# Fused attention and gated product on one core: a first set of plain block products, and weight work moved from GpSimd to VectorE

## The chip, the cores and the metric

The kernel runs on one core of a Trainium2 chip. The metric is the device time of one execution in microseconds (us). A core has a matrix engine (TensorE; PE in the profile, with its weight loads as PEld), three elementwise engines (VectorE or DVE, ScalarE or ACT, GpSimd or POOL) and SyncE (SP), whose queue issues most of the DMA transfers; ScalarE's queue can issue them too. Each engine takes its instructions in the order in which they were written, and they wait for each other by semaphores.

## The reference

Attention with a position bias comes first, then a gated product without a nonlinearity:

```python
def _attn_ref(q, k, v, w1, b1, w2):          # q, k, v: (8, 8, 576, 64)
    scores = scale * np.matmul(q, k.transpose(0, 1, 3, 2)) + bias(w1, b1, w2)
    attn = softmax(scores)
    return np.matmul(attn, v)
def _moe_ref(x, w1, w2, w3, w_out):          # x: (4608, 512)
    a = x @ w1                               # 512 x 1024
    b = x @ w2                               # 512 x 1024
    h = a * b @ w3                           # 1024 x 1024
    return h @ w_out                         # 1024 x 512
```

x is the attention's output, 8 x 576 tokens of 512 values. The change touches the second function alone.

## The kernel before, in words

**First half: attention** (to L592). 32 units, one for each pair of heads and batch, run one behind another in a periodic order written as tables of times. Each leaves its output in DRAM (`x_d`, L444) without the softmax's division; the reciprocals go to DRAM too (`r_d`, L357 and L358). Between the units the weights w_out and w3 are brought in. They come as 64-bit floats, and `narrow` (L144) makes 32-bit floats of them in eight steps: fetch (DMA into `wi`), size and rest (ScalarE), clamp, shift, head and power (VectorE: L172, L178, L188, L194), and total (L199 and L200, two tensor steps on GpSimd).

**The fold.** w3 and w_out are multiplied once on the core to one matrix of 1024 x 512 (`fold`, L630; 16 steps of 12 matmuls, L653). Numbers go to TensorE as a high and a low part, each in a form of reduced precision: high x high, high x low, low x high make three matmuls of one. ScalarE makes the high parts (a copy into that form), another engine the low part (the number less its high part). `evict_w` (L657) puts the results, again as high and low parts, where w3 was.

**Second half: six sets of 768 tokens** (`NPR` = 6, `TOK` = 768). A set's x (512 features x 768 tokens, `xr`) is loaded by `load_x` (L665), together with the reciprocals `rb` (L674), and scaled by `split_x` (L680): steps r0 to r3 scale, S1 to S4 are sums of quarters, h0 to h6 and l0 to l6 are seven high and low parts. Seven products take the place of eight (Winograd's form of Strassen's scheme for 2 x 2 blocks): the blocks are two halves of the tokens by two halves of the features on one side, and w1 and w2 by two halves of the features on the other. So the weights need four sums too (`sums_w`, L718, on GpSimd, 256 elements a partition each) and high and low parts of seven blocks (`split_w`, L725: high on ScalarE, low on GpSimd, L732, one step of 768 and one of 1024 elements).

A set has eight **turns**, one for each 128 of the 1024 columns (`NF` = 8), so there are 48 turns. In a turn TensorE makes the products P1, P2, P6, P5, P7, P3, P4 (`product`, L736; six matmuls of 384 columns each, L748) in two PSUM banks, and between them the six steps D0 to D5 of the turn before (`down`, L798; three matmuls of 512 columns, L805), which multiply with the folded matrix. `finish` (L757) copies and adds what stands in the banks (ScalarE L764, VectorE L767), multiplies both branches (g) and splits the result (gh on ScalarE L777, gl on VectorE). The weight sums and splits of turn n + 1 are made in turn n. Of the 16 weight pieces of w1 and w2 (`prep_w`, L611) six are made during the fold, the other ten in the first turns. At a set's first turn the set before is stored (`store`, L809): ScalarE copies a bank to one of two buffers (`wos6`, `wos7`), SyncE sends it.

**What sets the order.** Every step has a time in a plan (the constants at L26 to L57); `drive` (L205) sorts by it and writes the instructions of TensorE, ScalarE, VectorE and GpSimd in that order. On the chip only the order remains. SyncE's order is set by the scheduler, not by the plan.

Of the kernel before, what the change touches and what calls it, by code (L numbers as in the profile page):

```python
# [18 lines left out]
P = 128  # L19
# [27 lines left out]
L_X = 7 * STEP
ENDS_X = {
    "S3": L_X + 1.25, "S4": L_X + 2.90, "h2": L_X + 4.62, "l2": L_X + 5.60, "h3": L_X + 6.30, "l3": L_X + 7.40, "h4": L_X + 7.20,
    "l4": L_X + 9.65, "h5": L_X + 8.10, "l5": L_X + 11.50, "h6": L_X + 11.45, "l6": L_X + 12.70,  # L50
}
BEGIN_X = {"r0": 2.90, "r1": 4.70, "r2": 2.90, "r3": 4.70, "S1": 2.90, "S2": 4.70, "h0": 4.62, "h1": 6.30, "l0": 2.90, "l1": 4.70}
NEXT_X = (
    dict(ENDS_X, **{n: d + STEP * (3 + k // 2) for k, (n, d) in enumerate((n, BEGIN_X[n]) for n in ("r0", "r1", "r2", "r3", "S1", "S2", "l0", "l1"))},
         h0=5 * STEP + 6.3, h1=5 * STEP + 7.2),
    dict(ENDS_X, **dict(zip(("r0", "r1", "r2", "r3", "S1", "S2", "l0", "l1"), (5 * STEP + d for d in FREE_D))), h0=5 * STEP + 6.3, h1=5 * STEP + 7.2),
)  # L57
# [36 lines left out]
def relpos_attention_moe(  # L94
# [49 lines left out]
    def narrow(pool, src, n, x, queue, pieces=1, low=nc.scalar, both=True):  # L144
# [53 lines left out]
        def total():  # L198
            nc.gpsimd.tensor_tensor(x, x, f(d["power"]), op=ALU.mult)  # L199
            nc.gpsimd.tensor_tensor(x, d["mag"], x, op=ALU.add)  # L200
# [410 lines left out]
    def prep_w(pool, t, m):  # L611
# [18 lines left out]
    def fold(t, hf):  # L630
# [15 lines left out]
        (nc.gpsimd if hf and t % 2 else nc.vector).tensor_tensor(w3l, w3s[t][hf], f(w3h), op=ALU.subtract)  # L646
# [18 lines left out]
    def load_x(c, queue):  # L665

        X = sets[c]["X"] = xs.tile([P, NC, TOK], F32, name="xr", bufs=1)
        sets[c]["rb"] = []
        for cc in range(NC):
            queue.dma_start(X[:, cc, :], x_d[cc][:, c * TOK:(c + 1) * TOK])  # L670
# [301 lines left out]
```

## Time and profile before

| | |
|---|---|
| median of 3 runs | 1169.37 us (1169.08 to 1169.75) |
| profiled execution | 1172.74 us |
| its span, first to last instruction | 1171.0 us |
| mean granted clock of TensorE | 0.973 |
| busy: PE, DVE, ACT, POOL | 1089.6, 859.6, 697.6, 746.9 us |
| DMA over the span | 123.22 MB, mean 105 GB/s |

The page of the profile gives busy time by engine, a picture of the span in slices, the chain of work that ended last, and groups of instructions. A group's row names the source line, engine, operation, tiles (out<-in) and shapes, the count, the busy time, the mean duration in ns, and the idle time of the engine just before them with what ended it. A timeline's row gives the start and the duration in us; a bracket is idle time before it and what ended that. The table of windows gives busy time and count by engine in a stretch, then the granted clock, the share of DMA time and GB/s. A busy TensorE is not one at its peak, since pipelined matmuls overlap.

### The profile page before, as it was taken

What the parts mean: (1) busy time and instruction counts of PE and PEld (TensorE: products, weight loads), DVE (VectorE), ACT (ScalarE), POOL (GpSimd) and SP (SyncE); (2) the same over time, 40 slices, a digit from 0 to 9 for tenths busy, and PEclk for the clock granted to TensorE, in tenths of its full rate; (3) what the DMA queues carried; (4) which work ended last, traced back from release to release, by engine and by line L of the source; (5) the groups of instructions that cost most, each with busy time, mean ns of one, the idle gap of its engine ahead of it and who ended that gap; (6) DMA issues with size and microseconds to landing.
All of it is one profiled execution on the core that took longest, in us unless ns stands there. A gap on an engine that the chain in (4) does not pass through costs nothing.

```text
span 1171.0 us, 23840 instructions
## 1 busy us (share of the span) xinstructions
PE 1089.6 (93%) x9380; PEld 907.0 (77%) x9380; DVE 859.6 (73%) x1459; ACT 697.6 (60%) x1337; POOL 746.9 (64%) x542
## 2 busy tenths in 40 slices
PE   7769999999999999967788899999999999999997
PEld 3247778777777777645577789998998998999996
DVE  8948987997899799649699665784882784587333
ACT  6769988998998899633443263444354344335342
POOL 0337765775777576435789767785875776586750
PEclk9989999999999999988889899999999999999999
DMA  6954573556457354152221130121103103001001
GB/s 204 310 168 146 165 246 119 180 172 226 140 172 245 115 161 137 58 163 90 90 71 38 54 108 18 38 70 39 54 2 108 55 1 108 28 1 55 1 1 54
DMA packets 58159, 123.22 MB, mean 105 GB/s; under 512 B 9152, under 2 KB 19264, under 8 KB 58048
## 3 DMA queue, kind: packets, MB, share of 16 engines
q1 hardware_dynamic: 55568, 117.59, 31.8%
q10 hardware_dynamic: 2480, 4.11, 1.3%
q8 instruction: 74, 1.21, 0.4%
q14 instruction: 37, 0.30, 0.1%
HBM read 91.76 MB, written 29.92 MB: 104 GB/s over the span
## 4 chain that ended last, share of the span: by engine, by line
PE 74%; DMA 6%; POOL 4%; ACT 3%; DVE 3%; issue 2%; SPq 0%; ACTq 0%; DVEq 0%; POOLq 0%
PE up L748 26%; PE o L805 14%; PE pst L431 14%; PE s L311 12%; PE pst L368 6%; DMA out_dram<-wos 3%; DMA wi<-in_moe_w_dram 2%; POOL wt L723 2%; POOL wu L199 1%; POOL url L732 1%; DVE xr L693 1%; DMA x_d<-x 1%; DMA rb<-r_d 1%; PE wacc L653 1%; ACT pt L393 1%
## 5 line engine op out<-in xcount | busy, mean ns | idle before, releaser
L748 PE MATMUL up<-xch,urh 128*128 128x384 f32 x672 | 233.1, 347 | 24.6 <-ACT wos L764 14.8
L322 DVE CUSTOM_DVE_ANT_0 ts<-s,nb 128x576 f32<-128x576 f32 x288 | 210.7, 754 | 48.2 <-PE s L311 21.5
L748 PE MATMUL up<-xcl,urh 128*128 128x384 f32 x672 | 229.8, 342 | 0.0
L748 PE MATMUL up<-xch,url 128*128 128x384 f32 x672 | 229.5, 341 | 0.0
L347 ACT ACTIVATE pp<-ts,mx 128x576 f32<-128x576 f32 x256 | 195.8, 770 | 20.5 <-DVE mx L322 18.8
L767 DVE TENSOR_TENSOR wos<-up,wos 128x384 f32<-128x384 f32 x144 | 78.2, 551 | 171.3 <-PE up L748 160.6
L732 POOL TENSOR_TENSOR url<-wu,urh 128x768 fp32r<-128x768 f32 x48 | 90.5, 1886 | 151.7 <-ACT urh L734 151.7
L805 PE MATMUL o<-w3s,gh 128*128 128x512 f32 x576 | 183.5, 400 | 0.0
L431 PE MATMUL pst<-pt,rv 128*64 128x256 f32 (+1 forms) x1280 | 167.5, 407 | 1.6 <-DVE rt L391 1.4
L748 PEld LDWEIGHTS up<-xch,urh 128*128 128x128 f32 x672 | 128.7, 192 | 44.0 <-ACT wos L764 18.9
L777 ACT ACTIVATE gh<-g 128x384 fp32r<-128x384 f32 x96 | 50.5, 526 | 161.2 <-DVE g L767 159.8
L764 ACT COPY wos<-up 128x384 f32<-128x384 f32 x144 | 68.1, 477 | 118.9 <-PE up L748 118.9
L393 ACT ACTIVATE pt<-pst 128x1024 f32<-128x1024 f32 x128 | 124.0, 1018 | 21.6 <-PE pst L368 21.6
L748 PEld LDWEIGHTS up<-xch,url 128*128 128x128 f32 x672 | 128.6, 191 | 10.4
L431 PEld LDWEIGHTS pst<-pt,rv 128*64 128x64 f32 x1280 | 87.6, 136 | 63.2 <-issue 9.0
L732 POOL TENSOR_TENSOR url<-wt,urh 128x1024 fp32r<-128x1024 f32 x48 | 132.6, 2763 | 0.0
L311 PE MATMUL s<-kh,qh 64*128 64x288 f32 x640 | 118.5, 366 | 11.6 <-DVE mx L322 11.4
L748 PEld LDWEIGHTS up<-xcl,urh 128*128 128x128 f32 x672 | 128.2, 191 | 0.0
L805 PE MATMUL o<-w3s,gl 128*128 128x512 f32 x288 | 115.5, 401 | 0.4 <-DVE gl L767 0.4
L805 PEld LDWEIGHTS o<-w3s,gh 128*128 128x128 f32 x576 | 106.9, 191 | 4.9
L368 PE MATMUL pst<-ident,pp 64*128 64x64 f32 x2304 | 102.1, 223 | 0.8 <-ACT pt L393 0.8
L368 PEld LDWEIGHTS pst<-ident,pp 64*128 64x128 f32 x2304 | 97.0, 139 | 6.5 <-ACT pt L393 5.7
(105 smaller groups left out, 2261.8 us busy)
## 6 DMA issues: line engine op xcount, KB each, us to landing
rq<-in_q_dram SPq DMA_DIRECT2D x31, 640.0 KB
wi<-in_moe_w_dram SPq DMA_DIRECT2D x32, 512.0 KB
nb_d<-bev SPq DMA_DIRECT2D x36, 295.5 KB
rv<-in_v_dram SPq DMA_DIRECT2D x32, 320.0 KB
x_d<-x SPq DMA_DIRECT2D x32, 288.0 KB
rk<-in_k_dram SPq DMA_DIRECT2D x31, 288.0 KB
rb<-r_d SPq DMA_DIRECT2D x44, 192.0 KB
xr<-x_d SPq DMA_DIRECT2D x20, 384.0 KB
```

Of the source, the lines that this page charges most:

```text
L311: nc.tensor.matmul(s[:, hf, :HS], Q[x][rows, q0:q0 + P], K[y][rows, h * HS:(h + 1) * HS], start=(m == 0), stop=(m == len(ops) - 1),)
L322: nc.vector.tensor_tensor_reduce(out=halves(ts), in0=d.pop(("s", t))[:, :, :HS], in1=halves(NB[p, t]), op0=ALU.add, op1=ALU.min, scale=-1. ...
L347: nc.scalar.activation(pp, ts, AF.Exp, bias=mx, scale=-1.0, accum_out=sums[p][:, 9 * b + col:9 * b + col + 1])
L368: nc.tensor.transpose(ps[0:n, hf, c0:c0 + 64], x[rows], ident[rows, rows])
L393: nc.scalar.activation(o, x, AF.Copy)
L431: nc.tensor.matmul(o, x[:, c0:c0 + D], m, start=(c == 0), stop=(c == 4 and n_m == len(ms) - 1),)
L732: nc.gpsimd.tensor_tensor(l[:, rows], src, f(h[:, rows]), op=ALU.subtract)
L748: nc.tensor.matmul(acc, l[:, b, ks], r[:, k], start=(m == 0 and which in ("P1", "P2", "P5")), stop=(m == 3 * KH - 1), skip_group_check=whi ...
L764: nc.scalar.copy(d[name], d[src])
L767: nc.vector.tensor_tensor(o, a, b, op=op)
L777: nc.scalar.activation(d["gh"][:, i * CH:(i + 1) * CH], d["g"][:, i], AF.Copy)
L805: nc.tensor.matmul(d["o", t], l[:, sl], folded[ft][r], start=(ft == 0 and m == 0), stop=(ft == NF - 1 and m == 2),)
```

## The change

- The first set (c = 0, turns 0 to 7) is made of eight plain block products: `plain`, named A0, A1 (w1) and B0, B1 (w2) by token half, 12 matmuls of 384 columns each. It needs four high and low parts of x in place of seven, no sums of x or of weights, and weight splits of four blocks (1024 elements) in place of seven.
- `sums_w`, the low part in `split_w`, and `total` of the w1 and w2 pieces are on VectorE. All low parts of w3 in the fold are, too; GpSimd keeps those of w_out.
- Four weight pieces are made during the fold in place of six. The other twelve follow in the first turns at 0.6 and 7.6 us of a turn.
- The first x and r are loaded from SyncE's queue (before: ScalarE's), all four r at once, two of them into tiles that the sums of x use later.
- `store` goes through five buffers (`wos3` to `wos7`) in place of two. The copies in `finish` use three (`wos0` to `wos2`) in place of two sets of three.
- The tables of times are rewritten: when x of the next set is scaled, added and split, and where the weight steps stand in a turn.

The diff, cut to its core (the tables of times are shown by two lines):

```diff
-PROD, DOWN, STEP = 1.05, 0.682, 11.44
+FULL, HALF = 12.63, 11.57
+TURN_F = (("A0", 0.00), ("D0", 2.11), ("D1", 2.81), ("B0", 3.51), ("D2", 5.62), ("A1", 6.32), ("D3", 8.43), ("B1", 9.13), ("D4", 11.24), ("D5", 11.94))
...
         def total():
-            nc.gpsimd.tensor_tensor(x, x, f(d["power"]), op=ALU.mult)
-            nc.gpsimd.tensor_tensor(x, d["mag"], x, op=ALU.add)
+            add.tensor_tensor(x, x, f(d["power"]), op=ALU.mult)
+            add.tensor_tensor(x, d["mag"], x, op=ALU.add)
...
-        return narrow(cv, src, NC * P, x, nc.sync, pieces=NC)
+        return narrow(cv, src, NC * P, x, nc.sync, pieces=NC, add=nc.vector)
...
-        (nc.gpsimd if hf and t % 2 else nc.vector).tensor_tensor(w3l, w3s[t][hf], f(w3h), op=ALU.subtract)
+        nc.vector.tensor_tensor(w3l, w3s[t][hf], f(w3h), op=ALU.subtract)
...
         for cc in range(NC):
-            queue.dma_start(X[:, cc, :], x_d[cc][:, c * TOK:(c + 1) * TOK])
-            if cc < 2:
-                load_r(c, cc, queue)
+            nc.sync.dma_start(X[:, cc, :], x_d[cc][:, c * TOK:(c + 1) * TOK])
+            if cc < 2 or c == 0:
+                load_r(c, cc)
...
+        if c == 0 and cc > 1:
+            rb = xs.tile([P, KH, CH], F32, name=f"s{cc - 1}", bufs=1).rearrange("p k n -> p (k n)")
+        else:
+            rb = xs.tile([P, TOK], F32, name="rb", bufs=2)
...
-            nc.gpsimd.tensor_tensor(o, a, b, op=ALU.subtract)
+            nc.vector.tensor_tensor(o, a, b, op=ALU.subtract)
...
-        src, rows = ((B[:, 1:4], slice(0, 3)), (d["T"], slice(3, 7)))[part]
+        if n < NF:
+            src, rows = B, slice(0, 4)
+        else:
+            src, rows = (d["T"], slice(3, 7)) if part else (B[:, 1:4], slice(0, 3))
         if low:
-            nc.gpsimd.tensor_tensor(l[:, rows], src, f(h[:, rows]), op=ALU.subtract)
+            nc.vector.tensor_tensor(l[:, rows], src, f(h[:, rows]), op=ALU.subtract)
...
+    def plain(n, which):
+        d, x = turns[n], sets[0]["x"]
+        m, t = "AB".index(which[0]), int(which[1])
+        acc = d[which] = ps_up.tile([P, 512], F32, name=f"up{m}")[:, 0:CH]
+        wh, wl = d["w"]
+        for k in range(KH):
+            for j in range(KH):
+                b, js = 2 - 2 * m + k, slice(j * P, (j + 1) * P)
+                xh, xl = x[2 * t + k]
+                for i, (l, r) in enumerate(((wh, xh), (wl, xh), (wh, xl))):
+                    nc.tensor.matmul(
+                        acc, l[:, b, js], r[:, j], start=(k == j == i == 0), stop=(k == j == KH - 1 and i == 2),
+                    )
...
-        o = held.tile([P, DO], F32, name=f"wos{6 + t % 2}")
+        o = held.tile([P, DO], F32, name=f"wos{3 + (c * NT + t) % 5}")
...
-    add(later, end + 0.05, lambda: load_x(0, nc.scalar))
+    add(later, end + 0.05, lambda: load_x(0))
...
+    begin = [t_f + min(n, NF) * FULL + max(n - NF, 0) * HALF for n in range(NSTEP + 1)]
+    for i in range(len(EARLY_W), 2 * NF):
+        n, k = divmod(i - len(EARLY_W) + 1, len(FREE_W))
+        put_w(plan, wpool, i, begin[n] + FREE_W[k] - 6.0, begin[n] + FREE_W[k])
```

How instructions stand now, at three places. ScalarE around the load of the first x, before (`x` is the last attention output's copy, `xr` and `rb` the loads, `wmag` a weight piece, `w3h` the fold's high parts, `w3s<-wacc` the first folded results):

```order
L393 ACTIVATE x<-pst 128x320
L644 ACTIVATE w3h<-w3s_87 128x512
L670 DMA xr<-x_d_98 128x768
L678 DMA rb<-r_d_102 64x768 x2
L670 DMA xr<-x_d_99 128x768
L678 DMA rb<-r_d_103 64x768 x2
L670 DMA xr<-x_d_100 128x768
L670 DMA xr<-x_d_101 128x768
L162 ACTIVATE wmag<-wi 128x512
L166 ACTIVATE wu_9068<-wi 128x512
L644 ACTIVATE w3h<-w3s_74 128x512
```

The same place after the change:

```order
L397 ACTIVATE x<-pst 128x320
L648 ACTIVATE w3h<-w3s_87 128x512
L166 ACTIVATE wmag<-wi 128x512
L648 ACTIVATE w3h<-w3s_74 128x512
L664 ACTIVATE w3s_9438<-wacc_9108 128x512
```

The loads have left ScalarE's queue, and one weight step with them. On VectorE, a turn of the first set before (`wos<-up,wos` are the additions, `g` the products, `gl` the low parts, `wmag` and `wi` a weight piece):

```order
L767 TENSOR_TENSOR wos_9822<-up_9815,wos_9822 128x384
L188 SCALAR_TENSOR_TENSOR wmag<-wi,wmag 128x512
L194 TENSOR_SCALAR wi<-wmag 128x512
L172 TENSOR_SCALAR wmag<-wmag 128x512
L178 TENSOR_SCALAR wmag<-wmag 128x512
L767 TENSOR_TENSOR wos_9873<-up_9802,wos_9873 128x384
L188 SCALAR_TENSOR_TENSOR wmag<-wi,wmag 128x512
L767 TENSOR_TENSOR wos_9850<-up_9852,wos_9850 128x384
L767 TENSOR_TENSOR g<-wos_9822,wos_9850 128x384
L194 TENSOR_SCALAR wi<-wmag 128x512
```

And after (`wu` is the piece's total, `url` the low part of the next turn's weights):

```order
L790 TENSOR_TENSOR g<-up_9772,wos_9763 128x384
L790 TENSOR_TENSOR gl<-g,gh 128x384
L176 TENSOR_SCALAR wmag<-wmag 128x512
L182 TENSOR_SCALAR wmag<-wmag 128x512
L192 SCALAR_TENSOR_TENSOR wmag<-wi,wmag 128x512
L198 TENSOR_SCALAR wi<-wmag 128x512
L203 TENSOR_TENSOR wu_9634<-wu_9634,wi 128x512
L204 TENSOR_TENSOR wu_9634<-wmag,wu_9634 128x512
L790 TENSOR_TENSOR g<-up_9824,wos_9821 128x384
L790 TENSOR_TENSOR gl<-g,gh 128x384
```

A piece's four VectorE steps stand together now, with the two of its total behind them, and the three additions are gone. On VectorE, a turn of the other sets in which x of the next set is scaled, before:

```order
L767 TENSOR_TENSOR wos_10906<-up_10899,wos_10906 128x384
L693 TENSOR_TENSOR xr<-xr,rb 128x768 x2
L767 TENSOR_TENSOR wos_10951<-up_10887,wos_10951 128x384
L767 TENSOR_TENSOR wos_10931<-up_10933,wos_10931 128x384
L767 TENSOR_TENSOR g<-wos_10906,wos_10931 128x384
L767 TENSOR_TENSOR g<-up_10887,wos_10951 128x384
L767 TENSOR_TENSOR gl<-g,gh 128x384 x2
```

And after (`wt` are the weight sums):

```order
L790 TENSOR_TENSOR wos_10945<-up_10938,wos_10945 128x384
L730 TENSOR_TENSOR wt<-wu_9636 128x256 x2
L730 TENSOR_TENSOR wt<-wu_9636,wt 128x256 x2
L742 TENSOR_TENSOR url<-wu_9636,urh 128x768
L700 TENSOR_TENSOR xr<-xr,rb 128x768
L790 TENSOR_TENSOR wos_10986<-up_10930,wos_10986 128x384
L742 TENSOR_TENSOR url<-wt,urh 128x1024
L790 TENSOR_TENSOR wos_10968<-up_10972,wos_10968 128x384
L790 TENSOR_TENSOR g<-wos_10945,wos_10968 128x384
L790 TENSOR_TENSOR g<-up_10930,wos_10986 128x384
L790 TENSOR_TENSOR gl<-g,gh 128x384
```

The four sums and two low parts stand between the additions, and the scaling of x is spread, one step between two additions.

More of the change, by code (lines that the diff above doesn't have):

```diff
@@ L47 @@
[L47 to L50, printed above, removed]
-}
[L52 to L57, printed above, removed]
+AT_E = dict(a0=2.25, g0=5.80, h0=6.40, l0=7.00, a1=8.60, g1=11.40, h1=12.00, l1=12.65)
@@ L142, in relpos_attention_moe, with narrow @@
     MOST = struct.unpack("<f", struct.pack("<I", 0x47EFFFFF))[0]
-    def narrow(pool, src, n, x, queue, pieces=1, low=nc.scalar, both=True):
+    def narrow(pool, src, n, x, queue, pieces=1, low=nc.scalar, both=True, add=nc.gpsimd):
         d = {}
@@ L752, in product, with spare @@
                 m += 1
[L754 to L755 removed]
+    def spare(i):
+        return held.tile([P, DO], F32, name=f"wos{i}")[:, 0:CH]
     def finish(n):
         d = turns[n]
[L760 removed]
         def copy(name, i, src):
[L763 removed]
+            d[name] = spare(i)
             nc.scalar.copy(d[name], d[src])
@@ L831, in relpos_attention_moe @@
                 put(later, evict_w(hf * NF // 2 + n), at + PACE_F + 0.6 * n, at + PACE_F + 0.6 * n + 0.6)
-    for n in range(EARLY):
-        put_w(later, w01, n // 2, n % 2, t_s + AT_W1 + PACE_W * n)
+    for i, (fetch, at) in enumerate(zip(EARLY_F, EARLY_W)):
+        put_w(later, w01, i, t_s + fetch, t_s + at)
     drive([e for e in later if e[0] <= end])
@@ L839, in relpos_attention_moe @@
     psw.append(fo.enter_context(tc.tile_pool(name="psw1", bufs=1, space=PSUM)))
-    assert t_s + AT_F + NF * PACE_F > end
-    plan, t_f = [], t_s + AT_F + 2 * NF * PACE_F
+    assert t_s + AT_FO + NF * PACE_F > end
+    plan, t_f = [], t_s + AT_FO + 2 * NF * PACE_F
     def add(plan, at, step):
         plan.append((at, len(plan), step))
-    add(later, end + 0.05, lambda: load_x(0, nc.scalar))
-    at = max(t_s + AT_X, end + 0.1)
     def late(at, step):
         add(later if at < t_f - 0.5 else plan, at, step)
+    add(later, end + 0.05, lambda: load_x(0))
     for n, step in split_x(0).items():
-        late(max(t_s + AT_X, end + 0.1) + FIRST_X[n], step)
-    late(t_f - 9.0, lambda: sums_w(0))
-    for p in range(2):
-        late(t_f - 9.0 + AT_WH[p], lambda p=p: split_w(0, p, False))
-        late(t_f - 9.0 + AT_WL[p], lambda p=p: split_w(0, p, True))
+        if n in FIRST_X:
+            late(t_s + AT_X0 + FIRST_X[n], step)
+    for k in range(2):
+        late(t_f - AT_W0[1] + (0.0, 1.1)[k], lambda k=k: split_w(0, 0, k == 1))
     drive(later)
@@ L892, in relpos_attention_moe @@
         if ft == 0 and c + 1 < NPR:
-            add(plan, T + 10.0, lambda c=c: load_x(c + 1, nc.sync))
+            add(plan, T + 10.0, lambda c=c: load_x(c + 1))
+            table = NEXT_X if c else LAST_X
             for name, step in split_x(c + 1).items():
-                add(plan, T + NEXT_X[c == 0][name], step)
-    T = t_f + NSTEP * STEP
+                add(plan, begin[n + table[name][0]] + table[name][1], step)
+    T = begin[NSTEP]
     for t in range(NT):
```

126 lines of the change are left out of this document (61 added, 65 removed), and 6 rows, old and new, of tables (LAST_X, NEXT_X).

## The prediction

> **What bounds the kernel now.** First I cut the span into stages with the table of windows: attention's end with the first half of the weight fold, the fold's second half, the first eight turns, turns 8 to 46, the last turn and the tail.
>
> ```profile
> core 0: us, PE busy (x) PEld busy (x) DVE busy (x) ACT busy (x) POOL busy (x), PEclk, DMA share, GB/s
> 480.00:516.40 36.40, 33.94 (x198) 23.54 (x198) 20.41 (x28) 15.89 (x27) 21.17 (x16) 1.00 0.29 84
> 516.40:567.00 50.60, 30.99 (x97) 22.59 (x97) 31.51 (x36) 18.41 (x29) 24.97 (x18) 0.77 0.42 127
> 567.00:686.10 119.10, 99.88 (x464) 88.84 (x463) 102.11 (x106) 48.19 (x81) 97.02 (x68) 0.92 0.16 49
> 686.10:1148.70 462.60, 457.20 (x2341) 422.68 (x2340) 292.62 (x339) 198.55 (x333) 315.46 (x231) 0.99 0.13 43
> ```
>
> TensorE is nearly full in the first and fourth stage. In the second it works 31.0 of 50.6 us, at a granted clock of 0.77; in the third 99.9 of 119.1 us, at 0.92, while GpSimd is busy for 97.0. Those two stages and what keeps the fourth from being full are where time can go. TensorE's timeline has the edges (start, duration):
>
> ```profile
> 480.62 0.49 PE L653 MATMUL wacc<-woh,w3l 128*128 128x512 f32 x1
> ...
> 525.30 0.80 PE L653 MATMUL wacc<-woh,w3h 128*128 128x512 f32 x1 [8.72 <-ACT w3h L644]
> ...
> 538.04 0.80 PE L653 MATMUL wacc<-woh,w3l 128*128 128x512 f32 x1 [4.09 <-DVE w3l L646]
> ...
> 567.03 0.52 PE L748 MATMUL up<-xch,urh 128*128 128x384 f32 x1
> ...
> 686.08 0.33 PE L748 MATMUL up<-xch,urh 128*128 128x384 f32 x1
> ...
> 1148.74 0.33 PE L748 MATMUL up<-xch,urh 128*128 128x384 f32 x1
> ```
>
> Turn 0 starts at 567.03, turn 8 at 686.08, turn 47 at 1148.74. Idle time in brackets shows the fold waiting 8.72 us for ScalarE. Why ScalarE was late is in its own timeline:
>
> ```profile
> 480.00 0.68 ACT L162 ACTIVATE wmag<-wi 128x512 f32<-128x512 f32 x1 [0.80 <-DMA wi<-in_moe_w_dram]
> ...
> 522.41 0.99 ACTq L670 DMA_DIRECT2D xr<-x_d  x2
> 523.50 0.66 ACT L162 ACTIVATE wmag<-wi 128x512 f32<-128x512 f32 x1 [11.73 <-DMA x_d<-x]
> ```
>
> ScalarE's own queue held the loads of X, and those stood until the store of the last attention output had landed; 11.73 us of ScalarE went there. The chain of waits (start, length) gives the store, a pair of products, one fold step, an r load:
>
> ```profile
> 488.48 2.98 PE wacc L653 x12
> ...
> 514.18 8.88 DMA x_d<-x
> ...
> 531.63 4.33 DMA rb<-r_d
> ...
> 598.29 2.76 POOL wt L723 x3
> ...
> 714.96 2.11 PE up L748 x12
> ...
> 772.89 2.11 PE up L748 x12
> ```
>
> Five turns lie between the last two rows: (772.89 - 714.96) / 5 = 11.586 us is an undisturbed turn. Eight take 92.7 us; the first eight took 119.05, with GpSimd's steps on the chain.
>
> **The durations to use.** From the groups (mean ns), then VectorE's and GpSimd's timelines:
>
> ```profile
> L732 POOL TENSOR_TENSOR url<-wu,urh 128x768 fp32r<-128x768 f32 x48 | 90.5, 1886 | 151.7 <-ACT urh L734 151.7
> L732 POOL TENSOR_TENSOR url<-wt,urh 128x1024 fp32r<-128x1024 f32 x48 | 132.6, 2763 | 0.0
> L723 POOL TENSOR_TENSOR wt<-wu 128x256 f32<-128x256 f32 x96 | 90.6, 963 | 3.2
> L723 POOL TENSOR_TENSOR wt<-wu,wt 128x256 f32<-128x256 f32 x96 | 87.7, 913 | 3.8
> L767 DVE TENSOR_TENSOR wos<-up,wos 128x384 f32<-128x384 f32 x144 | 78.2, 551 | 171.3 <-PE up L748 160.6 <-ACT wos L764 10.6
> ```
>
> ```profile
> 530.99 2.04 DVE L693 TENSOR_TENSOR xr<-xr,rb 128x768 f32<-128x768 f32 x1
> ...
> 535.35 0.43 DVE L178 TENSOR_SCALAR wmag<-wmag 128x512 int32<-128x512 int32 x1
> ...
> 537.30 0.68 DVE L646 TENSOR_TENSOR w3l<-w3s,w3h 128x512 fp32r<-128x512 f32 x1
> 537.90 0.95 DVE L693 TENSOR_TENSOR xr<-xr,rb 128x768 f32<-128x768 f32 x1
> 538.77 0.69 DVE L188 SCALAR_TENSOR_TENSOR wmag<-wi,wmag 128x512 int32<-128x512 int32 x1
> ```
>
> ```profile
> 530.33 1.89 POOL L200 TENSOR_TENSOR wu<-wmag,wu 128x512 f32<-128x512 f32 x1
> 540.05 1.87 POOL L199 TENSOR_TENSOR wu<-wu,wi 128x512 f32<-128x512 f32 x1 [7.84 <-ACT xch L702]
> ```
>
> The same multiply of 768 elements takes VectorE 2.04 us while GpSimd works (530.33 to 532.22) and 0.95 us while GpSimd is idle (until 540.05). After the change GpSimd has nothing left once the fold's low parts of w_out are made, so I use the undisturbed values: 0.43, 0.69, 0.68 (512 elements), 0.95 (768). From 0.68 and 0.95 the slope is 0.27 per 256 elements; my estimates are 0.41 for 256 and 1.22 for 1024.
>
> The Trainium skill (SBUF — State Buffer, Who interferes with whom) says that VectorE and GpSimd share one port pair as an exclusive lock, so that the second to issue blocks. The 2.04 against 0.95 agrees; were the disturbed value to hold without GpSimd, first-set turns would be VectorE-bound at about 20 us and the time would be some 60 us above my sum.
>
> **Part 1: up to turn 0.** The second half of the fold now has X's loads on SyncE's queue, so ScalarE doesn't stop; the 8.72 us goes, the cold clock with it, and no weight sums or seven-part splits stand between fold and turn 0. What is late next is TensorE itself. It was nearly full up to 516.4. One new delay: the weight piece's first steps are now ahead of the first fold's low part on VectorE. ScalarE's 480.00 to 480.68 now comes before w3h; then 0.43 + 0.46 and a 0.36 copy (my estimate of what stands ahead), and w3l from about 482.0 to 482.7, against its matmul at 480.62 now: +2.1 us. So the first half ends at 518.5. The second half is 8 steps of 12 matmuls: at most 8 x 2.98 = 23.8, and about 0.17 less each for the pipelined last matmul, 22.5; I take 22.8. Turn 0 at 541.3: **-25.7 us**. Ends: -28 (no delay at the start) and -16 (X 10 us late, below).
>
> X itself: the last attention output is stored right behind the first X load, an estimated 2 us ahead of the present 514.18; with the 8.88 us of now it lands at 521, the last X and r loads take 4.33 more, so scaling ends near 528. VectorE's low part of fold step 5, queued behind the scaling, is wanted at 518.5 + 5 x 2.85 = 532.7. Cover 4 to 5 us; if it is gone, each further us is paid.
>
> **Part 2: first set.** Eight block products are 48 matmuls of 384 columns in place of 42. Twelve take 2.11 us at most, six 1.05; a turn is 11.586 + 1.05 = 12.64, eight 101.1 against 119.05: **-17.9 us**, if TensorE stays fed. VectorE per turn: two weight pieces of 3 x 0.43 + 0.69 + 2 x 0.68 = 3.34 each, one low part 1.22, two products and two low parts of 0.55: 6.68 + 1.22 + 2.2 = 10.1 of 12.64. In turns 4 to 7 the next set's X adds up to six steps of 0.95, where a piece or both are missing: about 12.3 in turn 6. GpSimd's load now per turn is 1.89 + 2.76 + 2 x (0.96 + 0.91) = 8.4, and each of ten late pieces adds about 3: 97 in 119 us, one step waiting for the other. The new piece steps don't feed the turn that they lie in, nor the next, so a late one costs nothing until it has used most of a turn. Ends: -17.9 and 0 (pieces pace the turns as now).
>
> **Part 3: the other 40 turns.** No matmul changes. VectorE per turn: seven steps of 0.55 (3.9), four sums (1.6), 0.95 and 1.22: 7.7 of 11.586; the 15 steps of the next X (scaling, sums, low parts) add at most three of 0.95 in one turn: 10.5, and 15 x 0.95 / 8 = 1.8 in the mean. By the turn's table P5, which needs the sum of P2 (due 2.35, 0.55 long), is due at 4.56, 1.6 us later; the next turn's P2, which needs the last product (due 10.40), has 1.6 us too. The new sums stand behind the first, and nothing longer than 1.22 stands before the second. I take 0. The ends: +2.5 us a turn if VectorE took GpSimd's times (3.9 + 8.4 + 1.8 = 14.1), and no gain.
>
> The stores do change this stage: 39 turns from 686.08 to 1148.74 take 462.66, against 451.9 undisturbed: 10.8 us too many. ScalarE's waits in this stage, and those in the tail:
>
> ```profile
> ACT wos L814 <- DMA out_dram<-wos: 22.7, 15, 4.6
> ```
>
> ```profile
> 1164.80 0.37 ACT L819 COPY wos<-o 128x256 f32<-128x256 f32 x1 [0.49 <-DMA out_dram<-wos]
> ...
> 1166.63 0.37 ACT L819 COPY wos<-o 128x256 f32<-128x256 f32 x1 [1.46 <-DMA out_dram<-wos]
> ```
>
> With two store buffers the third copy waits for the first transfer, and the copies of P1 queue behind it on ScalarE. With five, only the sixth copy reuses a buffer, 9.3 us after its first use (due 12.20 and 2.90); transfers of X that stand on SyncE's queue between the stores wait only for the last low part of the present X. I take 9.5 of the 10.8 as gone (0.25 stays at each of five set starts): **-9.5 us**, ends 0 and -10.8. In the tail 0.49 + 1.46: **-2.0 us**, ends 0 and -3.
>
> **The sum.** -25.7 - 17.9 - 9.5 - 2.0 = -55.1. The profiled execution took 1172.74 us (span 1171.0): 1117.6, span 1115.9. The median of the runs lies 3.4 lower, 1169.37: **1114.3 us**.
>
> **Rivals.**
> - X late. All X and r loads and the store go through one queue now. If that brings the last r 10 us beyond its cover, turn 0 starts at 551: 1124.3. For it: 8.88 us for one store with transfers ahead of it. Against: X of a set is 1.5 MB and the window moved 127 GB/s with room left. The Trainium skill (DMA: Bandwidth & Descriptors, Queues, rings and completion order) has descriptors of one queue consumed in ring order, which speaks against merging two queues; by that rule the wait is this rival's.
> - Pieces pace the first set. Load, ScalarE, six VectorE steps, next load into the same buffer is a loop over two buffers; if it turns in 15 us a pair as now, the 17.9 is not gained: 1132.2. Against: without GpSimd the loop has 10.1 us of VectorE in 12.64.
> - The store gaps stay, because the X loads between the stores hold SyncE: 1169.37 - 45.6 = 1123.8.
> - Slower: VectorE becomes the bound of the 40 turns. It decides above 11.586 + 55.1/40 = 13.0 us a turn; at 14.1 the time is 1114.3 + 40 x 2.5 = 1214. For it: in-order VectorE now holds everything between two products. Against: 7.7 by undisturbed rows.
> - That the work isn't moved: the order of instructions shows no GpSimd row after the fold, so no chance.
>
> **How the numbers follow.** Forecast 0.60, X late 0.14, pieces 0.13, store gaps 0.09, slower 0.03, no change 0.01. The range takes the forecast's ends on the good side (-28.2 - 17.9 - 10.8 - 3.0 = -59.9, 1109.5, less 1 for what these bounds leave out) and reaches to the pieces' rival: 1108.5 to 1133. 0.2% is 2.3 us, about what a measurement tells from no change; all cases but the last two are far faster. Faster 0.96, same 0.01, slower 0.03.
>
> **What would show it.** Right: the first product near 541, turn 8 about 101 us later at a clock of 1.00, turns of 11.59 at the set starts too, ScalarE without waits on the output's transfers, VectorE some 60 to 70% busy in the seven-product turns. Wrong: TensorE idle behind w3l (X late), VectorE's pieces waiting on loads with TensorE idle on url (pieces), or sums of P2 ending later than 1.6 us after P2 (VectorE-bound).

## The result and the profile after

| | before | after |
|---|---|---|
| median of 4 runs each, same chip | 1169.22 us (1167.12 to 1169.75) | 1115.74 us (1114.10 to 1116.05) |
| ratio, 95% interval | | 0.9543 (0.9526 to 0.9559) |
| profiled execution, its span | 1172.74, 1171.0 us | 1115.74, 1113.9 us |
| mean granted clock of TensorE | 0.973 | 0.989 |
| busy: PE, DVE, ACT, POOL | 1089.6, 859.6, 697.6, 746.9 us | 1076.3, 859.5, 688.3, 302.2 us |

The change is 4.6% faster, and the forecast of 1114.3 us is 1.4 us off. In three of the comparisons below one execution ran far longer than the rest (2605.5 and 3544.4 us, and 1473.1 us of the kernel before); the ratios leave these out, and no median moves by more than 0.7 us without them.

The table of windows of the changed kernel, cut at the same places as before (attention's end with the fold's first half, the second half, the first set, turns 8 to 46):

```profile
core 0: us, PE busy (x) PEld busy (x) DVE busy (x) ACT busy (x) POOL busy (x), PEclk, DMA share, GB/s
480.00:518.40 38.40, 35.43 (x223) 25.29 (x220) 22.63 (x36) 18.98 (x35) 11.08 (x8) 1.00 0.30 88
518.40:541.10 22.70, 21.61 (x93) 17.21 (x93) 16.43 (x24) 10.52 (x17) 0.00 (x0) 1.00 0.88 191
541.10:641.90 100.80, 98.18 (x511) 90.36 (x510) 82.48 (x134) 42.38 (x73) 0.00 (x0) 1.00 0.24 79
641.90:1093.80 451.90, 451.90 (x2342) 420.53 (x2341) 333.75 (x572) 200.75 (x332) 0.00 (x0) 1.00 0.13 44
```

GpSimd is at 0 from the fold's second half on, and the clock at 1.00 in all four rows. TensorE has no idle time left in the last row and 2.6 us in the third. VectorE does more in the first set than before (134 instructions against 106) in less busy time (82.48 us against 102.11). TensorE's timeline gives the edges and the waits that are left:

```profile
482.21 0.50 PE L657 MATMUL wacc<-woh,w3h 128*128 128x512 f32 x1 [1.16 <-ACT w3h L648]
...
483.83 0.50 PE L657 MATMUL wacc<-woh,w3l 128*128 128x512 f32 x1 [0.89 <-DVE w3l L650]
...
517.52 0.39 PE L657 MATMUL wacc<-woh,w3h 128*128 128x512 f32 x1
...
533.08 0.50 PE L657 MATMUL wacc<-woh,w3l 128*128 128x512 f32 x1 [1.09 <-DVE w3l L650]
...
541.10 0.34 PE L756 MATMUL up<-xch,urh 128*128 128x384 f32 x1
...
559.54 0.44 PE L756 MATMUL up<-xch,urh 128*128 128x384 f32 x1 [0.85 <-DVE g L790]
...
641.90 0.33 PE L772 MATMUL up<-xch,urh 128*128 128x384 f32 x1
...
1093.78 0.33 PE L772 MATMUL up<-xch,urh 128*128 128x384 f32 x1
```

The second half of the fold starts at 517.52, turn 0 at 541.10, turn 8 at 641.90, turn 47 at 1093.78. From first product to first product, turns 0 to 7 take 8.35, 13.70, 12.79, 12.79, 12.79, 13.69, 13.67 and 13.03 us; all 39 from turn 8 to 47 take 11.59. Set against the forecast's terms, in the profiled executions:

| term | forecast | measured |
|---|---|---|
| turn 0 | -25.7 | 567.03 to 541.10: -25.9 |
| first set | -17.9 | 119.05 to 100.80: -18.3 |
| turns 8 to 46 | -9.5 | 462.66 to 451.88: -10.8 |
| turn 47 and the tail | -2.0 | 22.26 to 20.12: -2.1 |
| sum | -55.1 | -57.1 |

Each term is within 1.3 us, but the first set's is right by luck, by two errors that cancel: turn 0 has no steps D0 to D5 to run and takes 8.35 us, not 12.64, and the next seven take 92.45, not 88.5. What VectorE does in a turn stands in its timeline, here one turn of the first set from low part to low part of the weights:

```profile
557.79 1.23 DVE L742 TENSOR_TENSOR url<-wu,urh 128x1024 fp32r<-128x1024 f32 x1 [1.13 <-ACT urh L744]
558.93 0.55 DVE L790 TENSOR_TENSOR g<-up,wos 128x384 f32<-128x384 f32 x1
560.07 0.56 DVE L790 TENSOR_TENSOR gl<-g,gh 128x384 fp32r<-128x384 f32 x1 [0.59 <-ACT gh L796]
...
565.29 0.56 DVE L790 TENSOR_TENSOR gl<-g,gh 128x384 fp32r<-128x384 f32 x1 [0.59 <-ACT gh L796]
...
570.58 1.23 DVE L742 TENSOR_TENSOR url<-wu,urh 128x1024 fp32r<-128x1024 f32 x1 [1.13 <-ACT urh L744]
```

570.58 - 557.79 = 12.79 us is the turn. Its work is 1.23 + 2 x (0.55 + 0.56) + 2 x 3.36 for the two pieces = 10.2, as forecast. The rest is waiting: twice 0.59, while ScalarE makes gh between VectorE's g and gl, and 1.13, while it makes urh between the total and url; that is 2.3, and 0.3 are small gaps. VectorE stands idle then, with the next piece's steps queued behind. So the reading is that VectorE's order, and not TensorE, sets these turns, by handshakes (the waits for ScalarE inside one chain) that the sum left out.

This turn and its like, turns 2 to 4, are only 0.2 us longer than the 12.61 that TensorE needs (experiment 1). Of the 4.2 us that the seven turns lose against that, 3.6 lie in the other four. Turns 5 and 6 have a scaling step of the next X on VectorE as well (0.95 us each, at 602.54 and 616.21), turn 7 more of them in place of the pieces; and behind turn 0, which TensorE is through with in 8.35 us, VectorE's list is late, and TensorE waits for g in turn 1 (0.85 us at 559.54).

### The profile page after: what moved, and what is told of

The parts are those of the page before. It is cut to its first block, busy times and chain, and to the rows that moved or that the text cites. A ratio compares the mean times of both kernels' runs of the same rounds, so it can differ in the third digit from the quotient of the medians.

```text
span 1113.9 us, 23788 instructions
## 1 busy us (share of the span) xinstructions
PE 1076.3 (97%) x9428; PEld 904.2 (81%) x9428; DVE 859.5 (77%) x1712; ACT 688.3 (62%) x1318; POOL 302.2 (27%) x218
## 4 chain that ended last, share of the span: by engine, by line
PE 80%; DVE 7%; ACT 3%; DMA 2%; issue 1%; ACTq 0%; SPq 0%; DVEq 0%
PE up L772 27%; PE o L828 15%; PE pst L435 15%; PE s L315 13%; PE pst L372 6%; PE wacc L657 2%; DVE url L742 1%; DMA s<-r_d 1%; DVE wu L203 1%; DVE wmag L192 1%; DVE g L790 1%; ACT gh L796 1%; DMA xr<-x_d 1%; ACT urh L744 1%; DVE gl L790 1%
## 5 line engine op out<-in xcount | busy, mean ns | idle before, releaser
L772 PE MATMUL up<-xch,urh 128*128 128x384 f32 x560 | 189.6, 338 | 0.0
L772 PE MATMUL up<-xcl,urh 128*128 128x384 f32 x560 | 189.2, 338 | 0.0
L772 PE MATMUL up<-xch,url 128*128 128x384 f32 x560 | 188.8, 337 | 0.0
L828 PE MATMUL o<-w3s,gh 128*128 128x512 f32 x576 | 180.6, 395 | 0.0
L790 DVE TENSOR_TENSOR wos<-up,wos 128x384 f32<-128x384 f32 x120 | 66.9, 558 | 99.2 <-PE up L772 99.2
L772 PEld LDWEIGHTS up<-xch,urh 128*128 128x128 f32 x560 | 105.2, 188 | 9.2
L772 PEld LDWEIGHTS up<-xch,url 128*128 128x128 f32 x560 | 105.1, 188 | 9.0
L772 PEld LDWEIGHTS up<-xcl,urh 128*128 128x128 f32 x560 | 105.0, 188 | 0.0
L315 PE MATMUL s<-kh,ql 64*128 64x288 f32 x640 | 96.8, 296 | 2.4 <-POOL ql L299 2.4
L315 PE MATMUL s<-kl,qh 64*128 64x288 f32 x640 | 96.1, 295 | 0.0
```

What stands on the lines that cost most here:

```text
L315: nc.tensor.matmul(s[:, hf, :HS], Q[x][rows, q0:q0 + P], K[y][rows, h * HS:(h + 1) * HS], start=(m == 0), stop=(m == len(ops) - 1),)
L772: nc.tensor.matmul(acc, l[:, b, ks], r[:, k], start=(m == 0 and which in ("P1", "P2", "P5")), stop=(m == 3 * KH - 1), skip_group_check=whi ...
L790: nc.vector.tensor_tensor(o, a, b, op=op)
L828: nc.tensor.matmul(d["o", t], l[:, sl], folded[ft][r], start=(ft == 0 and m == 0), stop=(ft == NF - 1 and m == 2),)
```

## The experiments

Theory: the time went where the forecast put it, with the first set bound by VectorE's handshakes. Rivals: that one edit alone does nearly all of it, or that the parts lean on each other. Times are medians; ratios, with 95% intervals, are to the kernel before, run on the same chip beside each.

### 1. Handshakes out of the first set

The changed kernel, with the weights' high and low part and both low parts of g later in the plan of a plain turn. On VectorE two low parts come to stand elsewhere, url behind a product and the second gl behind two steps of the next piece:

```diff
-AT_E = dict(a0=2.25, g0=5.80, h0=6.40, l0=7.00, a1=8.60, g1=11.40, h1=12.00, l1=12.65)
+AT_E = dict(a0=2.25, g0=5.80, h0=6.40, l0=7.20, a1=8.60, g1=11.40, h1=12.00, l1=13.70)
-AT_RF = dict(h=3.00, l=4.20)
+AT_RF = dict(h=4.50, l=6.50)
```

> The changed kernel with VectorE's and ScalarE's order in the first set altered: the weights' low part comes behind the product g0, and the second low part of g behind the first two steps of the next piece, so that ScalarE makes the high parts while VectorE does something else. Theory: VectorE's loop falls from 12.79 to about 10.6 us a turn, TensorE becomes the bound at 12.64, and turns 1, 5, 6 and 7 lose their excess: 4 us less, 1111.5 to 1113 us. Rival, the excess comes from elsewhere (loads, TensorE itself): no change.

1111.16 us (ratio 0.9507, 0.9484 to 0.9531). Turns 1 to 7 take 12.59 to 12.61 us each, and in the table of windows the first set has TensorE full:

```profile
540.10:636.70 96.60, 96.60 (x511) 90.94 (x510) 81.28 (x136) 43.34 (x74) 0.00 (x0) 1.00 0.26 83
```

In VectorE's timeline of this kernel, the low part of g now stands behind two steps of a piece:

```profile
573.94 0.55 DVE L790 TENSOR_TENSOR g<-up,wos 128x384 f32<-128x384 f32 x1
575.63 0.43 DVE L176 TENSOR_SCALAR wmag<-wmag 128x512 f32<-128x512 f32 x1 [1.14 <-ACT wmag L166]
576.10 0.43 DVE L182 TENSOR_SCALAR wmag<-wmag 128x512 int32<-128x512 int32 x1
576.44 0.55 DVE L790 TENSOR_TENSOR gl<-g,gh 128x384 fp32r<-128x384 f32 x1
```

gl no longer waits. Over the set VectorE's waits of gl fall from 8.9 us to 0.6 and those of url from 6.3 to 2.0. VectorE still has idle time elsewhere, but it is no longer what TensorE waits for. The set shrinks from 100.80 to 96.62 us with the same instructions in another order, and turns 1, 5, 6 and 7 lose their excess with the rest; that shows the handshakes as the cause. 12.61 is also the forecast's 12.64 for a turn in which TensorE is fed. Of the 5.2 us between the two spans, 4.2 are this; the other 1.0 is that turn 0 starts at 540.08, for which experiment 2 has the reason. This version is faster than both kernels.

### 2. The fold's first step as well

The same kernel, with the first weight piece of the fold 0.6 us later in the plan, since TensorE's first fold step had waited behind it:

```diff
-EARLY_W = 1.0, 6.0, 21.0, 44.0
+EARLY_W = 1.6, 6.0, 21.0, 44.0
```

> As the run before, and the first weight piece's steps come behind the first fold step's high and low part on ScalarE and VectorE. Theory: the first half of the fold starts 2 us earlier and TensorE carries that through: another 2 us less, 1109.5 to 1111 us. Rival, TensorE waits for something else in the fold's first half: no further change.

1111.46 us (0.9505, 0.9480 to 0.9531): no further gain. In TensorE's timeline of this kernel:

```profile
480.54 0.50 PE L657 MATMUL wacc<-woh,w3h 128*128 128x512 f32 x1 [0.29 <-ACT w3h L648]
...
487.38 2.86 PE L435 MATMUL pst<-pt,rv 128*64 128x320 f32 x20 [2.00 <-DVE rt L395]
...
516.75 0.40 PE L657 MATMUL wacc<-woh,w3h 128*128 128x512 f32 x1
...
532.09 0.50 PE L657 MATMUL wacc<-woh,w3l 128*128 128x512 f32 x1 [0.88 <-DVE w3l L650]
```

The fold starts earlier, and the attention step behind it waits 2.00 us. Its second half still starts 0.8 us earlier than in experiment 1 (517.57), and gives that back at 532.09, where the low part waits 0.88 behind the scaling of X. The changed kernel shows this wait as 1.09 at 533.08, and experiment 1, where X's last r happened to land 1.0 us earlier, not at all. So in these three runs X's arrival decides turn 0 to within a microsecond.

### 3. The moved work alone

The kernel before, with the totals, sums and all low parts on VectorE; seven products in the first set, X from ScalarE's queue, two store buffers and the tables stay:

```diff
-        return narrow(cv, src, NC * P, x, nc.sync, pieces=NC)
+        return narrow(cv, src, NC * P, x, nc.sync, pieces=NC, add=nc.vector)
...
-        (nc.gpsimd if hf and t % 2 else nc.vector).tensor_tensor(w3l, w3s[t][hf], f(w3h), op=ALU.subtract)
+        nc.vector.tensor_tensor(w3l, w3s[t][hf], f(w3h), op=ALU.subtract)
...
-            nc.gpsimd.tensor_tensor(o, a, b, op=ALU.subtract)
+            nc.vector.tensor_tensor(o, a, b, op=ALU.subtract)
...
-            nc.gpsimd.tensor_tensor(l[:, rows], src, f(h[:, rows]), op=ALU.subtract)
+            nc.vector.tensor_tensor(l[:, rows], src, f(h[:, rows]), op=ALU.subtract)
```

> The kernel before with the move alone: totals of the w1 and w2 pieces, weight sums, weights' low parts and all low parts of w3 on VectorE, everything else (seven products in the first set, tables, six early pieces, x from ScalarE's queue, two store buffers) as before. Theory: five turns of the first set hold two pieces and the seven-product work on VectorE, 6.7 + 7.7 = 14.4 us and waits for ScalarE, about 15.5 us a turn, and the stall of the fold stays: 1154 to 1164 us. Rival, the move alone brings most of the gain: 1135 us or less.

1137.35 us (0.9729, 0.9701 to 0.9757), outside both and close to the rival. The move brings 32 of the 53.5 us: turn 8 starts at 659.94 instead of 686.08, and turns 8 to 46 take 452.4 instead of 462.7 us, though two store buffers are left. One reason stands in SyncE's queue. Of the kernel before:

```profile
506.42 7.66 SPq L157 DMA_DIRECT2D wi<-in_moe_w_dram  x2
514.18 0.46 SPq L444 DMA_DIRECT2D x_d<-x  x1
```

The first row of SyncE's waits between 505 and 515 us (in total, times, longest):

```profile
SPq L157 <- POOL wu L199: 13.6, 2, 6.8
```

The copy of the last attention output was done at 511.26 (it starts at 510.82 and takes 0.44). Its store left SyncE only at 514.18, since a weight load ahead of it waited until GpSimd had made a total. With the totals on VectorE, SyncE and ScalarE read:

```profile
514.03 0.34 SPq L444 DMA_DIRECT2D x_d<-x  x1
515.89 0.37 SPq L157 DMA_DIRECT2D wi<-in_moe_w_dram  x1
```

```profile
513.57 0.44 ACT L393 ACTIVATE x<-pst 128x320 f32<-128x320 f32 x1 [7.58 <-PE pst L431]
...
519.39 0.66 ACT L162 ACTIVATE wmag<-wi 128x512 f32<-128x512 f32 x1 [4.85 <-DMA rb<-r_d]
```

The store now leaves right behind its copy, and the weight load comes behind the store in SyncE's order. It doesn't leave earlier (514.03 against 514.18), since the copy itself is 2.75 us later. But ahead of it went one load of X, where two of X, four of r and the weight load had gone before, and the chain of waits has it land after 4.20 us in place of 8.88:

```profile
514.03 4.20 DMA x_d<-x
```

ScalarE stands for 4.85 us where it had stood for 11.73; 2.8 of the difference is that it starts to wait later, 4.1 that it goes on earlier (519.39 against 523.50). On TensorE the wait at this place falls from 8.72 to 1.90 us, with X's loads in ScalarE's queue as before:

```profile
521.17 0.50 PE L653 MATMUL wacc<-woh,w3h 128*128 128x512 f32 x1 [1.90 <-ACT w3h L644]
```

The window from the first product to turn 8 says what bounds the rest:

```profile
550.57:659.90 109.33, 99.91 (x486) 87.39 (x487) 101.77 (x186) 52.51 (x89) 0.00 (x0) 0.98 0.21 68
```

VectorE is busy for 101.77 of 109.33 us. This window is not the first set alone: the six matmuls of its first product stand among the fold's last two steps, and these run until 557.90. Measured from there, the fold is done 9.1 us earlier than before (567.03), and 17.0 us are won between the fold's end and turn 8.

### 4. All but the plain products

Experiment 3 with the first x and r on SyncE's queue and five store buffers:

```diff
-    add(later, end + 0.05, lambda: load_x(0, nc.scalar))
+    add(later, end + 0.05, lambda: load_x(0, nc.sync))
...
-        o = held.tile([P, DO], F32, name=f"wos{6 + t % 2}")
+        o = held.tile([P, DO], F32, name=f"wos{3 + (c * NT + t) % 5}")
...
-        return held.tile([P, DO], F32, name=f"wos{i + 3 * (n % 2)}")[:, 0:CH]
+        return held.tile([P, DO], F32, name=f"wos{i}")[:, 0:CH]
```

> The kernel before with the weight steps and low parts on VectorE (as in the run with the move alone: 1137.35, turn 0 at 550.57, first set 109.4 us), and now also with the first x and r on SyncE's queue and with five store buffers: all of the change but the eight plain products, their tables and the four early pieces. Theory (each part has its own price, and the plain products bring what is left): turn 0 comes 3 to 6 us earlier, as ScalarE's wait of 4.85 us goes, the set starts give 1 to 2 us and the tail 2, so 1127 to 1132, 11 to 16 us above the full change, of which about 8.6 is the longer first set with sums and seven splits and the rest the later turn 0. Rival (the plain products bring little, queue and buffers do the rest): under 1121. A second rival (X's loads on SyncE come late without the tables of the change): 1136 or more, no gain.

1133.53 us (0.9711, 0.9694 to 0.9728), between the theory and its second rival. Turn 8 starts at 659.99, as without these edits: the queue brings nothing here; the tail is 1.9 us shorter. SyncE's and then ScalarE's timeline:

```profile
519.65 2.13 SPq L670 DMA_DIRECT2D xr<-x_d  x2
521.88 0.53 SPq L157 DMA_DIRECT2D wi<-in_moe_w_dram  x1
```

```profile
531.25 0.66 ACT L162 ACTIVATE wmag<-wi 128x512 f32<-128x512 f32 x1 [8.72 <-DMA wi<-in_moe_w_dram]
```

Six weight pieces are still made during the fold. A piece's load leaves SyncE behind X's loads, by 522.41, and ScalarE goes on only at 531.25, when it has landed; it waits 8.72 us for it. TensorE's longest wait in the second half of the fold is as long as in experiment 3 and has only changed its name; there, and then here:

```profile
534.71 0.80 PE L653 MATMUL wacc<-woh,w3l 128*128 128x512 f32 x1 [5.94 <-DVE w3l L646]
```

```profile
533.04 0.80 PE L653 MATMUL wacc<-woh,w3h 128*128 128x512 f32 x1 [5.92 <-ACT w3h L644]
```

In the full change only four pieces are early. Of the 17.8 us that are left to 1115.74, all lies ahead of turn 8 (659.99 to 641.90): the plain products with their tables and the four early pieces. Most of it is not in the turns: here too turn 0's first product stands among the fold's last steps, which run until 558.13, and the full change has the fold done at 541.10. From there to turn 8 it is 101.86 us here, the first product already made, and 100.80 in the full change. Which of the three edits gets the fold done 17 us earlier, no run shows.

### 5. Store buffers: five alone, and two in the full change

Five buffers in the kernel before (the second and third edit of experiment 4), then two in the changed kernel:

```diff
-        o = held.tile([P, DO], F32, name=f"wos{3 + (c * NT + t) % 5}")
+        o = held.tile([P, DO], F32, name=f"wos{6 + t % 2}")
```

> The kernel before with five store buffers (and one set of three copy buffers) alone. Theory: the excess at the set starts, 10.8 us, and 2 us of the tail go: 1156 to 1158 us. Rival, GpSimd's disturbance is the cause: 1167 us or more.

> The changed kernel with two store buffers in place of five. Theory: the copies wait for the output's transfers again, 10.8 us over the turns at the set starts and 2 in the tail: 1128 us, with ScalarE's waits on output transfers near 23 us. Rival, the long turns at the set starts came from GpSimd's and VectorE's disturbance: no change, 1115 to 1117 us.

Five alone: 1160.47 us (0.9928, 0.9902 to 0.9953), 2.5 above the theory. Turns 9, 17, 25 and 33 fall to 11.59 us; the first turn of each set keeps 11.8, which is 11.59 with the moved work (experiment 3). Two in the changed kernel: 1121.83 us (0.9598, 0.9564 to 0.9632), 6.1 us above it and between theory and rival. Its profiled execution took 1125.03 us, with 6.8 us too many in the same four turns, 2.1 in the tail, and two waits back in ScalarE's list (us in total, times, longest):

```profile
ACT wos L837 <- DMA out_dram<-wos: 13.5, 5, 3.5
ACT wos L842 <- DMA out_dram<-wos: 2.9, 2, 1.5
```

So the buffers are worth about 9 us to the kernel before and 6 to 9 to the changed one (by medians and by profiled executions), and nearly nothing in the turns of experiments 3 and 4 (0.5 between them). The gap needs two things: a third copy that needs the first buffer again, and a store that lands late. Experiment 6 asks why it does.

### 6. The stores in a queue of their own

The kernel before at the start of set 3, turn 24 from 873.80, in SyncE's queue:

```profile
877.22 2.61 SPq L670 DMA_DIRECT2D xr<-x_d  x3
879.88 0.43 SPq L815 DMA_DIRECT2D out_dram<-wos  x1
```

and on ScalarE:

```profile
880.21 0.59 ACT L814 COPY wos<-o 128x512 f32<-128x512 f32 x1
885.40 0.59 ACT L814 COPY wos<-o 128x512 f32<-128x512 f32 x1 [4.59 <-DMA out_dram<-wos]
```

Three loads of X (384 KB each) go out just ahead of the first store, which lands 5.5 us after its issue. The test sends the stores from ScalarE:

```diff
             nc.scalar.copy(o, acc)
-            nc.sync.dma_start(rows, o)
+            nc.scalar.dma_start(rows, o)
```

> The kernel before, with the output of sets 0 to 4 sent from ScalarE's queue in place of SyncE's; two store buffers as before. Theory (at a set start in the kernel before up to three loads of X of 384 KB are issued just ahead of the first store in the same queue, 877.22 to 879.83 ahead of 879.88, and the store lands only at 885.4, behind them): from another queue the first transfer lands in about 3 us, ScalarE's waits on it fall from 22.7 us to 10 or less, and the excess at turns 9, 17, 25 and 33 from 10.8 us to 4 or less: 1161 to 1165. Rival (the loads and the store share the same engines and memory, whatever the queue): the waits stay at 18 us or more and the time within 3 us of before, 1167 to 1172, or above if ScalarE's issues of 0.3 to 0.6 us delay its copies.

1177.90 us (1.0094, 1.0071 to 1.0117), slower; the rival held. ScalarE's list of waits:

```profile
ACT wos L814 <- DMA out_dram<-wos: 21.5, 9, 5.4
```

It was 22.7 in all, and the excess at the set starts grew from 10.8 to 16.5 us. At the same set start all four loads leave SyncE between 883.14 and 885.49, the store leaves ScalarE at 885.06, and the third copy goes on at 889.72, 4.7 us later. So the order within one queue is not the cause by itself: with loads and stores of one moment in two queues, the store still takes 4.7 us, where 5.5 were taken in one queue and 3.1 in experiment 3. The Trainium skill (DMA: Bandwidth & Descriptors, Queues, rings and completion order) says that each transfer engine takes turns between the queues that have work for it, and that SyncE's and ScalarE's queues use the same sixteen; this run agrees in that the other queue doesn't spare the store its wait. In experiment 3 the stores and loads alternate in SyncE's queue, two loads and then one between two stores, and the first store lands in 3.1 us. That order is not enough either: with two buffers in the changed kernel (experiment 5) loads and stores alternate too, and a store issued at 747.16 holds the copy two further on until 752.73. Why the issues fall as they do is the scheduler's order, which no run varied by itself.

### 7. Weight totals, or sums and low parts, back on GpSimd

In the changed kernel, one moved part at a time:

```diff
-        return narrow(cv, src, NC * P, x, nc.sync, pieces=NC, add=nc.vector)
+        return narrow(cv, src, NC * P, x, nc.sync, pieces=NC, add=nc.gpsimd)
```

> The changed kernel with the two last steps of each w1 and w2 piece on GpSimd again. Theory: the first set is bound by VectorE's loop of 12.79 us (10.1 busy, the rest waits for ScalarE's high parts); it loses 2.8 us of work and gains a wait of up to 2.6 us and some disturbance, so the time stays within 3 us: 1113 to 1119 us. Rival, GpSimd's totals paced the first set before: about 15 us a turn, 1130 us or more.

1121.68 us (0.9593, 0.9561 to 0.9626), 6 above the changed kernel, between theory and rival. Turn 0 comes at 538.81, 2.3 us earlier: with two steps of each piece fewer on VectorE, the fold's second half starts 0.9 us earlier (516.60) and runs without the wait at 533.08. The first set then takes 107.1 us; ScalarE's and TensorE's waits in it:

```profile
ACT urh L744 <- POOL wu L204: 27.6, 6, 5.7
```

```profile
PE up L756 <- DVE g L790: 7.5, 6, 2.3
```

Here a late piece does cost: ScalarE waits for the total, VectorE for ScalarE's high part, and g stands behind that on VectorE.

The second kernel puts the sums and the low parts back from turn 8 on:

```diff
-            nc.vector.tensor_tensor(o, a, b, op=ALU.subtract)
+            nc.gpsimd.tensor_tensor(o, a, b, op=ALU.subtract)
...
-            nc.vector.tensor_tensor(l[:, rows], src, f(h[:, rows]), op=ALU.subtract)
+            (nc.gpsimd if n >= NF else nc.vector).tensor_tensor(l[:, rows], src, f(h[:, rows]), op=ALU.subtract)
```

> The changed kernel with the weight sums and the weights' low parts of the seven-product turns on GpSimd again (the first set stays on VectorE). Theory: TensorE sets these turns at 11.59 us with either engine, so no change: 1114 to 1118 us. Rival, moving this work is worth something in all 40 turns: at 0.25 us a turn 10 us, 1126 us or more.

1117.27 us (0.9551, 0.9513 to 0.9588), not to be told from the changed kernel; turn 8 takes 12.52 us, turns 9 to 46 take 11.59 each. From there on it is all the same who does this work, with five buffers in place.

### 8. The first X back on ScalarE's queue

```diff
-            nc.sync.dma_start(X[:, cc, :], x_d[cc][:, c * TOK:(c + 1) * TOK])
+            (nc.sync if c else nc.scalar).dma_start(X[:, cc, :], x_d[cc][:, c * TOK:(c + 1) * TOK])
...
-            nc.sync.dma_start(rb[rows], r_d[cc][h:h + 1, c * TOK:(c + 1) * TOK].broadcast_to([64, TOK]))
+            (nc.sync if c else nc.scalar).dma_start(rb[rows], r_d[cc][h:h + 1, c * TOK:(c + 1) * TOK].broadcast_to([64, TOK]))
```

> The changed kernel with one part undone: the first set's x and r are loaded from ScalarE's queue again. Theory: the 8.72 us stall of the fold had two causes, the queue and a late store of the last attention output (held up by the early weight pieces). Now that store is issued near 512 and lands near 519, so ScalarE is blocked until about 519 only, TensorE wants the next high part at 518.5, and the second half of the fold starts 1 to 4 us late: 1117 to 1120 us. Rival, the queue alone made the stall: 9 us or more, 1124 us or over.

1122.50 us (0.9605, 0.9568 to 0.9642), 6.8 above the changed kernel, between theory and rival. ScalarE, then TensorE:

```profile
520.25 0.66 ACT L170 ACTIVATE wu<-wi 128x512 f32<-128x512 uint32 x1 [6.81 <-DMA rb<-r_d]
```

```profile
521.48 0.80 PE L657 MATMUL wacc<-woh,w3h 128*128 128x512 f32 x1 [3.81 <-ACT w3h L648]
```

The wait is 3.81 us, at the upper end of what was expected. But the matmul behind it takes 0.80 instead of 0.39: the granted clock is 0.5 for 6.8 us from 520.4 on. With that, turn 0 comes 6.1 us late (547.19).

## Why the prediction was right, and where only its sum was

**Up to turn 0** (-25.7; measured -25.9). ScalarE's wait and the cold clock went, as said. The first fold step waited for w3h and w3l as expected, and the first half ended at 517.52 and not 518.5. X was mis-sized: "scaling ends near 528" became 532.42 (the last scaling in VectorE's timeline starts at 531.46 and takes 0.96). The store of the last attention output was quicker than the 8.88 us taken over for it: it left at 512.45 and, as X's loads read it, had landed when the last of them left at 518.68. But the loads behind it took far more than "4.33 more". The last r left at 521.57, and the chain of waits has it on the way for

```profile
521.57 9.77 DMA s<-r_d
```

The rival's counter-argument, 127 GB/s "with room left", no longer held: in the second half of the fold the DMA engines were busy for 0.88 of the time, at 191 GB/s. The cover was used up and 1.09 us paid. The rival X late was there, at a tenth of its price. The first half's earlier end (1.0 us) and fold steps of 2.77 us, where 2.85 was taken, made up for it.

**The credit for that term** was given to the queue. Experiment 8 shows that it is worth 6.1 us in the full change, and experiment 4 shows nothing without the rest of it. In experiment 3 TensorE's wait falls from 8.72 to 1.90 us with the queue as it was; there the store is no longer held behind a weight load that waits for GpSimd. The prediction read the 8.88 us of that store as a transfer's time and didn't ask why it was issued 2.9 us after its copy.

**First set** (-17.9; -18.3). The step that failed is the condition "if TensorE stays fed", held to be met because VectorE has 10.1 us of work in 12.64 and a late piece "costs nothing until it has used most of a turn". The sum added VectorE's durations and left out its waits for ScalarE between steps of one chain, 2.3 us a turn, and where the next X's steps come on top, VectorE is the bound. It is the rival "Pieces pace the first set", at a quarter of its price. Experiment 1 takes most of these waits away and finds the 12.61. The error of +4.0 was hidden by turn 0, which has no D steps (-4.3); that the term came out is luck. Nor do the plain products earn it alone: with seven products, the move by itself wins 17.0 us between the fold's end and turn 8 (experiment 3), though there the first product and some of turn 0's other work fall into the fold. The VectorE estimates themselves hold: 1.23 for 1024 elements, 0.42 for 256, 0.95 for 768.

**Turns 8 to 46** (-9.5; -10.8). "I take 0" for the moved work held as to VectorE's capacity: 333.75 busy in 451.9 us. As to the stores it didn't. In the kernel before, the move alone closes the gaps almost wholly (experiment 3, 0.5 us left), the 0.2 us at each set start included that the forecast had kept, and five buffers close most of them by another way. In the changed kernel the move is not enough: with two buffers 6.8 us come back (experiment 5). So the buffers earn most of the term there, as forecast, and the total was right because the change has both.

**Tail** (-2.0; -2.1). As forecast: two buffers in the changed kernel bring 2.1 us back, and experiments 3 and 4 differ by 1.9 us behind turn 47.

**The median.** The forecast took 3.4 us off the profiled time; after the change the profiled execution is the median. A sum 2.0 us too cautious and 3.4 us that did not recur leave the forecast 1.4 us low.

## What to carry to other kernels

An engine's share of busy time is not its room: where its in-order list goes to another engine and back inside one chain (0.59 and 1.13 us here), either put independent steps between, or count the waits as its work. When moving work off a slow engine, look for queues that wait on that engine (here SyncE's loads), since what stands behind them moves too (4.1 us of the fold's gain in experiment 3). Edits that cure the same wait don't add up: do each alone before giving it the credit.

## What the runs showed of the hardware

VectorE's busy time is the same in both kernels (859.6 and 859.5 us), although 445 us of GpSimd work went, most of it to VectorE. The groups by form in turns 8 to 46 show a part of why. Before:

```profile
L767 DVE TENSOR_TENSOR wos<-up,wos 128x384 f32<-128x384 f32 x117 | 63.3, 552 | 150.6 <-PE up L748 140.0 <-ACT wos L764 10.6
...
L693 DVE TENSOR_TENSOR xr<-xr,rb 128x768 f32<-128x768 f32 x16 | 43.8, 2776 | 0.0
...
L767 DVE TENSOR_TENSOR g<-wos,wos 128x384 f32<-128x384 f32 x39 | 32.8, 842 | 1.3
```

After:

```profile
L790 DVE TENSOR_TENSOR wos<-up,wos 128x384 f32<-128x384 f32 x117 | 65.2, 558 | 92.2 <-PE up L772 92.2
...
L790 DVE TENSOR_TENSOR g<-wos,wos 128x384 f32<-128x384 f32 x39 | 21.8, 558 | 1.4
...
L700 DVE TENSOR_TENSOR xr<-xr,rb 128x768 f32<-128x768 f32 x16 | 15.2, 951 | 0.0
```

Beside a busy GpSimd, a step with both inputs in SBUF (xr, and g from two wos) is slower in the mean, 2776 against 951 ns and 842 against 558; one with an input in PSUM (up) is not, 552 against 558. The Trainium skill (SBUF — State Buffer, Who interferes with whom) states just this split for VectorE's two-input operations; the trace agrees. With the sums and low parts back on GpSimd (experiment 7), xr took 1667 ns and g 770 again, hidden in turns that TensorE bounds.

The clock costs more than its wait: in experiment 8, the 3.81 us of an idle TensorE end at 521.48, and the clock stays at half until 527.2: 5.7 us at half speed are up to 2.9 us more of lost work.
